# One full transpose per unit from a table that holds the weights twice, and merges in 32 pieces

## The chip, the core and the metric

The kernel is one program on one core of a Trainium2 chip. The core has five engines that run their own instruction streams and meet at semaphores: PE (TensorE, matrix products), DVE (VectorE), ACT (ScalarE), POOL (GpSimd) and SP (SyncE, which here only issues transfers). Sixteen DMA engines move data between the main memory and the core's own memory. The metric is the device time of one execution in microseconds (us). In the profile PEld is the loading of a stationary operand into PE, a queue written as POOLq or PEq is the sequencer of that engine, and `L1238` is line 1238 of the kernel's file.

## The reference, cut to what matters

Three layers follow each other over 14336 tokens of 192 numbers: a short causal convolution (softmax weights over 7 taps, one set of weights per head), a soft mixture of experts, and a sparse mixture in which every token goes to its two best of eight experts.

```python
x = attn(x, weight)                       # 7 taps per head, group of 24 columns
logits = x @ phi                          # 32 slots
slot_input = softmax_over_tokens(logits).T @ x
slot_out = relu(slot_input[e] @ w1[e]) @ w2[e]        # 8 experts, 4 slots each
x = softmax_over_slots(logits) @ slot_out             # = c @ slot_out
noisy = x @ w_gate + log1p(exp(x @ w_noise)) * noise
top2 = the two largest of the 8 per token; top2_w = their softmax
for e in range(8):                                    # second mixture
    h = relu(x[tokens of e] @ moe2_w1[e])             # 192 -> 1024
    out[tokens of e] += top2_w * (h @ moe2_w2[e])     # 1024 -> 192
```

After the first mixture a token is known by its 32 slot weights `c` alone, since `x = c @ slot_out`. The kernel uses that: `x @ moe2_w1[e]` becomes `c @ (slot_out @ moe2_w1[e])`, a product over 32 slots. To keep precision with 16-bit operands, `c` and the folded weights are each split into a high and a low half (hi, lo), so a product over 32 slots has 4 x 32 = 128 rows: hi·hi, lo·hi, hi·lo and lo·lo.

## The kernel before, in words

**Prefix (0 to about 146 us).** Eight groups of 16 x 112 tokens pass through the convolution, the transposes, the logits and the slot sums (`conv`, `trans`, `logits`, `slotsum`). The slot weights of every token stay in the tile `call` (112 partitions, 128 x 32 numbers). The small experts of the first mixture close the prefix.

**Routing of set 0 (about 146 to 188 us).** The tokens form four sets of 3584. For set 0 `route` works out, mostly on DVE, which tokens go to which expert at which place. In the middle ACT and POOL fill the tile `tab`, in four parts (`s_hi`): ACT copies the high halves from `call`, POOL subtracts for the low halves. In between ACT and POOL also fold and split the weights of the second mixture (`w1_split`, tiles `whl`, then `W1P`). `s_st` stores `tab` as rows of `table` in main memory. A row is 33 numbers: 32 numbers' worth of hi and lo halves, and one gate. Each token has two rows, one for its first and one for its second expert, with the same hi and lo and another gate.

**Units (from about 188 us).** The work on experts is cut into 238 units of 128 tokens with one expert. Each unit runs through these steps:

- `gather(i)`: POOL issues an indirect transfer that brings 128 rows of `table` (line 1183). It is issued 10 to 20 units ahead.
- `fetch(i)`: SP issues the load of the expert's first weights, 256 KB.
- `prep(i)`: PE transposes the 128 rows twice (line 1205), into PSUM partitions 0 to 63 and 64 to 127, since the 128-row product needs hi and lo twice. ACT copies the result to `ct`.
- `layer1(i)`: eight PE products (line 1214), then ACT makes the high half `hh` (line 1218) and DVE the low half `hl` (line 1219).
- `layer2(i)`: sixteen PE products, a 384-column one from `hh` (line 1227) and a 192-column one from `hl` (line 1229) in turn, then ACT and DVE scale by the gate and add (lines 1235, 1236) into one of five `o` tiles.
- POOL issues an indirect transfer that scatters `o` to one of two output arrays (line 1238): first experts to `out_0`, second experts to `out_1`, in turn.

PE, ACT, DVE, POOL and SP run their units' steps in program order. The routing of the sets 1 to 3, and of a last group MIX of partly filled units, is threaded between the units, a few DVE steps per unit by a budget. Whatever is left of a set's routing when its first gather is due is put there in one piece. The order of the units is set 0, 1, 2, MIX, 3.

**Merges.** At the end `out_1` must be added to `out_0`. POOL issues accumulating transfers from memory to memory (line 1305). Before the change there are eight, two per set, each of 1344 KB. The first six stand after the units 197, 203, 209, 215, 221 and 227; the two of set 3 stand after the last unit. Gathers, scatters and merges share POOL's instruction stream and one DMA queue. A scatter waits for the landing of the previous scatter to the same output, which is the one two units before.

Of the kernel before, what the change touches and what calls it, by code (L numbers as in the profile page):

```python
# [21 lines left out]
F32 = mybir.dt.float32  # L22
F16 = mybir.dt.float16
# [32 lines left out]
ROW = 33  # L56
CW = 32
# [9 lines left out]
MLAG, MSTEP, MPARTS = 2, 6, 2  # L67
# [21 lines left out]
def kernel(ctx, tc, xh, wraw_in, wband_in, consts_in, phi_in, w1a_in, w1b_in, w2_in, wgn_in, noise_in,  # L89
# [7 lines left out]
    table = dram.tile([2 * (NTOK + 128), ROW], F32, name="table")  # L97
# [35 lines left out]
    wrb = keep.tile([128, 4, 16], F32, name="wrb")  # L133
    ct0 = [keep.tile([128, 4 * P], F32, name=f"ct0{i}") for i in range(len(SETS[0]))]
# [110 lines left out]
    def v_split(e, half):  # L245
        w = W2[:, e * 3072:(e + 1) * 3072].rearrange("p (k d) -> p k d", k=8)[:, 4 * half:4 * half + 4]
        v = V2[e][:, 4 * half:4 * half + 4]
        t = v2t[half]
        DVE.tensor_scalar(t, v, w2s[:, e:e + 1], None, op0=OP.mult)
        if half:  # L250
            POOL.tensor_scalar(w[:, :, :D], v, w2s[:, e:e + 1], None, op0=OP.mult)
        else:
            ACT.activation(w[:, :, :D], t, AF.Copy)  # L253
        POOL.tensor_tensor(out=w[:, :, D:], in0=t, in1=w[:, :, :D], op=OP.subtract)  # L254

# [145 lines left out]
    def load_small():  # L401
        SP.dma_start(noise, noise_in)
        SP.dma_start(wgn, wgn_in)
        for o in outs:
            SP.dma_start(o[NTOK:], zero[:, :D])
        SP.dma_start(table[2 * NTOK:].rearrange("(p k) r -> p (k r)", k=2), zero[:, :2 * ROW])

# [5 lines left out]
    for g in range(NG):  # L413
        last = g == NG - 1
        conv(g, (0, 1, 2, 3))
        if g:
            tok_e(g - 1)
        if not g:
            v_stat(0)
        conv(g, (4, 5))  # L420
        if not g:
            v_max(0)
        if 0 < g < NG - 1:
            tok_l(g - 1)
        conv(g, (6, 7))
        if g + 2 < NG:
            load_x(g + 2)
        else:
            load_w1_rest(g - NG + 2)
        if g:  # L430
            v_rest(g)
            if g + 2 < NE:
                load_v(g + 2)
        trans(g, TPART[0])
        if not g:
            v_rest(0)
# [215 lines left out]
    def route(s, pool, rbank, idbank, nb):  # L652
# [46 lines left out]
        def s_hi(gl, h):  # L699
            if gl == 0 and h == 0:  # L700
                R["tab"] = pool.tile([P, TT, 2, ROW], F32, name="tab", bufs=1)
            a, b = gl * GT + h * GT // 2, gl * GT + (h + 1) * GT // 2
            tv = R["tab"].bitcast(F16)[:, a:b, :, :2 * CW].rearrange("p j c (b s) -> p j c b s", b=2)
            c2 = call[:, g0 + a:g0 + b, :].unsqueeze(2).to_broadcast([P, b - a, 2, NS])
            a = ACT.activation(tv[:, :, :, 0, :], c2, AF.Copy)
            if s:
                tc.keep_in_program_order(a)
            (DVE if s else POOL).tensor_tensor(out=tv[:, :, :, 1, :], in0=c2, in1=tv[:, :, :, 0, :], op=OP.subtract)
# [116 lines left out]
        def s_g3(i):  # L825
# [5 lines left out]
            DVE.tensor_tensor(out=R["tab"][:, :, i, CW], in0=f, in1=R["gd"][:, 2 - i], op=OP.mult)  # L831

        def s_st(gl):
            a = 2 * (TROW[s] + gl * GT * P) * ROW
            dst = bass.AP(tensor=table.tensor, offset=table.offset + a, ap=[[2 * GT * ROW, P], [1, 2 * GT * ROW]])
            SP.dma_start(dst, R["tab"][:, gl * GT:(gl + 1) * GT].rearrange("p j c w -> p (j c w)"))
# [103 lines left out]
        def s_ids():  # L940
# [11 lines left out]
            for c in range(2):  # L952
                DVE.tensor_scalar(R["row"][:, c], x[:, c, :N], 2.0, c - 2.0, op0=OP.mult, op1=OP.add)
# [51 lines left out]
    def route_mix(pool, bank):  # L1005
# [104 lines left out]
        def x_ids():  # L1110
# [7 lines left out]
            for c in range(2):  # L1118
                DVE.tensor_scalar(R["row"][:, c], a[:, c], 2.0, c - 2.0, op0=OP.mult, op1=OP.add)
# [60 lines left out]
    def gather(i):  # L1180
        s, c, u = order[i]
        RW[i] = fin.tile([128, ROW], F32, name="row", bufs=LOOK + RAMP[1] + 2)
        POOL.indirect_dma_start(out=RW[i], out_offset=None, in_=table[:2 * TEND[s]],  # L1183
# [37 lines left out]
    def layer2(i):  # L1221
# [9 lines left out]
        gv = RW[i][:, CW:]  # L1231
# [151 lines left out]
```

## Time and profile before

| what | value |
|---|---|
| time, median of 3 runs | 921.35 us (917.63 to 921.68) |
| profiled execution, its own time | 924.08 us |
| span of the profiled execution | 922.2 us |
| mean granted PE clock, of 2.4 GHz | 0.957 |
| PE busy | 841.6 us, 91% |
| DVE / ACT / POOL busy | 623.7 / 512.7 / 544.9 us |

A busy share is an average over the whole span. PE busy is close to the span because its products are pipelined and overlap in the record. POOL's 59% leaves out the gaps between its instructions. A row of the timeline gives start, duration, engine, line, the operand names, a count when rows are merged, and in square brackets the idle time before with what ended it.

### The profile page before, as it was taken

To read this page: it belongs to the slowest core of one execution; us is meant where nothing else is said; L and a number is where in the kernel's file an instruction comes from. 1 tells how busy PE (TensorE), PEld (TensorE's weight loads), DVE (VectorE), ACT (ScalarE), POOL (GpSimd) and SP (SyncE) were. 2 spreads that over 40 slices of the span, in tenths; PEclk is the share of its full clock that TensorE was granted. 3 is DMA by queue.
4 is the path that set the end of the run, shared out by engine and by line. 5 is a ranking of instruction groups with operands and counts; after the bars stand their busy time and mean duration, and the time that the engine had idled before them with its cause. 6 is when DMAs were issued, how large, how long until landed. Compare 5 with 4: busy or idle time off the path is not lost. (4 is left out here: it accounts for less than half of the span.)

```text
span 922.2 us, 25241 instructions
## 1 busy us (share of the span) xinstructions
PE 841.6 (91%) x8187; PEld 586.0 (64%) x8187; DVE 623.7 (68%) x1362; ACT 512.7 (56%) x1064; POOL 544.9 (59%) x534
## 2 busy tenths in 40 slices
PE   9999999399999999999999989999999897878960
PEld 5655544267777777776777767777776675655740
DVE  4768655959897989788989896665655564444530
ACT  5656524356577757766675535656555554444530
POOL 2354332277676767667776617777777775655431
PEclk9999999599999999999999989999999999888985
DMA  8675395643445343544364314444444346666646
GB/s 318 223 278 180 109 405 230 184 147 133 133 128 179 133 140 123 180 138 138 101 210 135 132 64 149 138 149 136 144 137 139 127 148 172 164 159 160 167 95 128
DMA packets 63702, 148.85 MB, mean 161 GB/s; under 512 B 13008, under 2 KB 20880, under 8 KB 61024
## 3 DMA queue, kind: packets, MB, share of 16 engines
q1 hardware_dynamic: 42624, 108.78, 32.0%
q0 software_dynamic: 20960, 38.46, 17.7%
q8 instruction: 79, 1.29, 0.6%
q14 instruction: 39, 0.32, 0.1%
HBM read 56.34 MB, written 39.47 MB: 104 GB/s over the span
## 5 line engine op out<-in xcount | busy, mean ns | idle before, releaser
L1227 PE MATMUL po<-W,hh 128*128 x1904 | 495.6, 330 | 24.5 <-DVE o L1236 24.4
L1229 PE MATMUL po<-W,hl 128*128 x1904 | 471.1, 249 | 0.0
L1219 DVE SCALAR_TENSOR_TENSOR hl<-ph,hh 128x1024 f16<-128x1024 f32 (+1 forms) x240 | 291.0, 1213 | 102.3 <-ACT hh L1218 100.0
L1238 POOL DMA_INDIRECT out_dram<-o,ids x238 | 240.8, 1012 | 136.5 <-DVE o L1236 65.1
L1183 POOL DMA_INDIRECT row<-table,row x238 | 232.1, 975 | 109.6 <-issue 45.1
L1218 ACT ACTIVATE hh<-ph 128x1024 f16<-128x1024 f32 (+1 forms) x240 | 243.7, 1016 | 41.2 <-PE ph L1214 16.2
L1227 PEld LDWEIGHTS <-hh 128*128 128x128 f16 x1904 | 188.1, 99 | 110.9 <-issue 5.6
L1235 ACT ACTIVATE t<-po,row 128x192 f32<-128x192 f32 x238 | 99.8, 419 | 239.8 <-PE po L1229 221.4
L1229 PEld LDWEIGHTS <-hl 128*128 128x128 f16 x1904 | 188.0, 99 | 27.8 <-issue 27.1
L1236 DVE SCALAR_TENSOR_TENSOR o<-po,row,t 128x192 f32<-128x192 f32 x238 | 98.9, 415 | 106.2 <-DMA out_dram<-o,ids 74.7
L1214 PE MATMUL ph<-ct,ws 128*128 128x128 f16 x1904 | 149.4, 222 | 1.6 <-DVE hl L1219 0.8
L1214 PEld LDWEIGHTS <-ws 128*128 128x128 f16 x1904 | 108.5, 98 | 17.7 <-issue 1.6
L1207 ACT ACTIVATE ct<-pt 128x128 f16<-128x128 f16 x238 | 64.0, 269 | 7.1 <-PE pt L1205 6.6
L254 POOL TENSOR_TENSOR W<-m,W 128x768 f16<-128x768 f32 x16 | 26.4, 1648 | 69.4 <-ACT W L253 68.7
L1205 PE MATMUL pt<-id,row 128*64 128x128 f16 x476 | 59.3, 245 | 0.2 <-DMA row<-table,row 0.2
L1205 PEld LDWEIGHTS <-row 128*64 128x64 f16 x476 | 26.2, 107 | 51.1 <-issue 38.0
L276 PE MATMUL cv<-arena,m 118*112 118x384 f32 x112 | 41.0, 495 | 0.0
L924 ACT ACTIVATE ohu<-ohu,cst 112x72 f16<-112x72 f16 x118 | 32.2, 343 | 14.7 <-DVE ohu L908 13.1
L276 PEld LDWEIGHTS cv<-arena,m 118*112 118x112 f32 x112 | 17.9, 176 | 13.7 <-issue 3.4
L293 PE MATMUL t<-cst,y 112*128 112x112 f32 x192 | 22.2, 264 | 0.6 <-ACT x1t L296 0.6
L318 ACT ACTIVATE ets<-lt,mg 128x448 f32<-128x448 f32 x8 | 5.1, 633 | 31.3 <-DVE mg L317 27.1
L282 DVE COPY y<-cv 112x384 f32<-112x384 f32 (+2 forms) x32 | 13.9, 454 | 12.3 <-PE cv L276 8.4
(327 smaller groups left out, 689.0 us busy)
## 6 DMA issues: line engine op xcount, KB each, us to landing
ws<-W1P SPq DMA_DIRECT2D x238, 256.0 KB
arena<-in_xh_dram SPq DMA_DIRECT2D x7, 1536.0 KB
out_dram<-out_dram POOLq DMA_DIRECT2D x8, 1344.0 KB
arena<-in_v_dram SPq DMA_DIRECT2D x8, 768.0 KB
arena<-in_w1a_dram SPq DMA_DIRECT2D x4, 1024.0 KB
arena<-in_v1a_dram SPq DMA_DIRECT2D x2, 2048.0 KB
row<-table,row POOLq DMA_INDIRECT x238
out_dram<-o,ids POOLq DMA_INDIRECT x238
```

The costliest lines, as they stand in the source:

```text
L276: PE.matmul(cvv, T[:, h, :], X[g][:, :, h * GC:(h + 1) * GC], start=True, stop=True)
L1183: POOL.indirect_dma_start(out=RW[i], out_offset=None, in_=table[:2 * TEND[s]], in_offset=bass.IndirectOffsetOnAxis(ap=RT[s]["row"][:, c, u ...
L1205: PE.transpose(pt[a:a + 64, :128], RW[i][:, :CW].bitcast(F16), id16)
L1207: ACT.activation(CT[i], pt[:, :128], AF.Copy)
L1214: L1[i] = PE.matmul(ph[:, k * 128:(k + 1) * 128], WS[i][:, k * 128:(k + 1) * 128], CT[i], start=True, stop=True).ins
L1218: ACT.activation(HH[i][:, s], ph[:, s], AF.Relu)
L1219: LO[i] = DVE.scalar_tensor_tensor(HL[i][:, s], ph[:, s], 0.0, HH[i][:, s], op0=OP.max, op1=OP.subtract).ins
L1227: PE.matmul(po[:, :384], HH[i][:, k * 128:(k + 1) * 128], w[:, bass.ds(r, 384)], start=k == 0, stop=False, skip_group_check=True)
L1229: last = PE.matmul(po[:, 192:384], HL[i][:, k * 128:(k + 1) * 128], w[:, bass.ds(r, 192)], start=False, stop=k == 7, skip_group_check=True)
L1235: PIN[ET.Activation] = ACT.activation(t, po[:, :D], AF.Copy, scale=gv).ins
L1236: PIN[ET.DVE] = DVE.scalar_tensor_tensor(o, po[:, D:2 * D], gv, t, op0=OP.mult, op1=OP.add).ins
L1238: POOL.indirect_dma_start(out=dst, out_offset=bass.IndirectOffsetOnAxis(ap=RT[s]["ids"][:, c, u:u + 1], axis=0), in_=o, in_offset=None)
```

## The change

**The table.** A row now has 66 numbers and there is one row per token: hi, lo, hi, lo, and both gates. The table keeps its size. The row numbers for the gathers are the token numbers, without the factor two. The gate of a unit is column `CW + c` of the row.

**The transpose.** `prep` makes one 128 x 128 transpose instead of two of 128 x 64.

**The low halves of set 0.** A new tile `hilo0` holds hi and lo of set 0. It is filled by `hi_lo` in the prefix, in the groups 2 and 3. In the routing of set 0, `s_hi` is one ACT copy per part that writes hi, lo, hi, lo, and POOL has no part in it. It stands after four of the dense steps instead of after one. For the sets 1 to 3 the number and size of the instructions of `s_hi` stay the same.

**The merges.** 32 pieces of 336 KB instead of 8 of 1344 KB: eight per set, one every 1.6 units from unit 197 on, and the eight of set 3 after the last unit.

```diff
-ROW = 33
-CW = 32
+ROW = 66
+CW = 64
-MLAG, MSTEP, MPARTS = 2, 6, 2
+MLAG, MSTEP, MPARTS = 2, 1.6, 8
+    hilo0 = keep.tile([P, NSET[0] // P, 2, NS], F16, name="hilo0")
+    def hi_lo(a, b):
+        ACT.activation(hilo0[:, a:b, 0, :], call[:, a:b, :], AF.Copy)
+        POOL.tensor_tensor(out=hilo0[:, a:b, 1, :], in0=call[:, a:b, :], in1=hilo0[:, a:b, 0, :], op=OP.subtract)
...
         if 0 < g < NG - 1:
             tok_c(g - 1)
+        if 2 <= g < 2 + len(SETS[0]):
+            hi_lo((g - 2) * GT, (g - 1) * GT)
...
+            if s == 0:
+                tv = R["tab"].bitcast(F16)[:, a:b, :2 * CW].rearrange("p j (a r) -> p j a r", a=2)
+                ACT.activation(tv, hilo0[:, a:b].rearrange("p j b s -> p j (b s)").unsqueeze(2)
+                               .to_broadcast([P, b - a, 2, 2 * NS]), AF.Copy)
+                return
...
-            (DVE if s else POOL).tensor_tensor(out=tv[:, :, :, 1, :], in0=c2, in1=tv[:, :, :, 0, :], op=OP.subtract)
+            DVE.tensor_tensor(out=tv[:, :, :, 1, :], in0=c2, in1=tv[:, :, :, 0, :], op=OP.subtract)
...
-            for c in range(2):
-                DVE.tensor_scalar(R["row"][:, c], x[:, c, :N], 2.0, c - 2.0, op0=OP.mult, op1=OP.add)
+            DVE.tensor_scalar(R["row"], x[:, :, :N], -1.0, None, op0=OP.add)
...
-            while parts and (k == 0 if s == 0 else len(parts) >= len(dense) - k):
-                add(s_hi, 0.0 if s == 0 else 0.6, *parts.pop(0))
+            while len(parts) >= len(dense) - k or (parts and s == 0 and k >= 3):
+                add(s_hi, 0.6 if s else 0.0, *parts.pop(0))
...
-            for a in (0, 64):
-                PE.transpose(pt[a:a + 64, :128], RW[i][:, :CW].bitcast(F16), id16)
+            PE.transpose(pt[:, :128], RW[i][:, :CW].bitcast(F16), id16)
...
-        gv = RW[i][:, CW:]
+        gv = RW[i][:, CW + c:CW + c + 1]
...
-            merges.setdefault(min(when, NU - 1), []).append((a + k * NSET[s] // MPARTS, a + (k + 1) * NSET[s] // MPARTS))
+            merges.setdefault(min(int(when), NU - 1), []).append((a + k * NSET[s] // MPARTS, a + (k + 1) * NSET[s] // MPARTS))
```

The change shows in the program order at three places. The first is PE, at the seam between the second layer of one unit and the first layer of another (`hl` and `hh` are the halves of the hidden numbers, `row` the gathered rows, `ws` the expert's weights). Before:

```order
L1229 MATMUL po<-W_66,hl 128x192
L1205 LDWEIGHTS row
L1205 MATMUL pt<-id_71,row 64x128
L1205 LDWEIGHTS row
L1205 MATMUL pt<-id_71,row 64x128
L1214 LDWEIGHTS ws
L1214 MATMUL ph<-ct,ws 128x128
```

Of the change, whose lines stand nine further down:

```order
L1238 MATMUL po<-W_66,hl 128x192
L1214 LDWEIGHTS row
L1214 MATMUL pt<-id_71,row 128x128
L1223 LDWEIGHTS ws
L1223 MATMUL ph<-ct,ws 128x128
```

Two loads and two products with 64 output rows became one load and one product with 128, the shape of its neighbours.

The second place is POOL in the routing of set 0, between the end of the prefix (`call`) and the first gathers (`row<-table`). Before:

```order
L353 TENSOR_TENSOR call<-call,rs 112x512 x2
L630 TENSOR_TENSOR whl<-wt,whl 128x512 x2
L708 TENSOR_TENSOR tab<-call,tab 112x16x32 x4
L630 TENSOR_TENSOR whl<-wt,whl 128x512 x2
L828 TENSOR_TENSOR u<-sb,fe 112x256
```

Of the change:

```order
L359 TENSOR_TENSOR call<-call,rs 112x512 x2
L638 TENSOR_TENSOR whl<-wt,whl 128x512 x4
L840 TENSOR_TENSOR u<-sb,fe 112x256
```

The four subtractions for `tab` left this place; two subtractions for `hilo` stand in the prefix instead.

The third place is the end of POOL's stream, from the last gather on (`out_dram<-o` are scatters, `out_dram<-out_dram` merges). Before:

```order
L1183 DMA row<-table,row_2207 128x33
L1238 DMA out_dram<-o,ids_2206 3584x192 x4
L1305 DMA out_dram<-out_dram 224x1536
L1238 DMA out_dram<-o,ids_2206 3584x192 x6
L1305 DMA out_dram<-out_dram 224x1536
L1238 DMA out_dram<-o,ids_2206 3584x192 x10
L1305 DMA out_dram<-out_dram 224x1536 x2
```

Of the change:

```order
L1193 DMA row<-table,row_2207 128x66
L1247 DMA out_dram<-o,ids_2206 3584x192 x2
L1314 DMA out_dram<-out_dram 64x1344
L1247 DMA out_dram<-o,ids_2206 3584x192
L1314 DMA out_dram<-out_dram 64x1344
...
L1247 DMA out_dram<-o,ids_2206 3584x192
L1314 DMA out_dram<-out_dram 64x1344
L1247 DMA out_dram<-o,ids_2206 3584x192 x4
L1314 DMA out_dram<-out_dram 64x1344 x8
```

Twenty scatters follow the last gather in both. Before, two merges stand among them and four stand ahead of the last gather; now ten stand among them and fourteen ahead.

## Rows read from the trace of the kernel before

**Rows 1.** Windows: stretches; busy us of each engine (instructions), granted clock, DMA share, GB/s.

```profile
194.50:527.10 332.60, 330.50 (x3347) 245.37 (x3347) 288.79 (x688) 224.64 (x480) 237.62 (x236) 1.00 0.44 144
527.10:548.75 21.65, 18.02 (x204) 13.53 (x202) 21.29 (x69) 6.55 (x12) 0.03 (x1) 0.84 0.12 44
548.75:769.00 220.25, 216.99 (x2092) 155.59 (x2091) 130.02 (x162) 129.03 (x241) 167.66 (x172) 1.00 0.43 141
769.00:844.00 75.00, 61.72 (x535) 42.97 (x533) 32.07 (x41) 33.10 (x63) 45.07 (x46) 0.89 0.67 162
844.00:902.40 58.40, 43.31 (x380) 30.26 (x377) 23.32 (x31) 22.46 (x42) 21.45 (x22) 0.90 0.54 137
```

**Rows 2.** Timeline of PE, a unit's second layer ends and another's first layer begins.

```profile
401.45 0.33 PE L1227 MATMUL po<-W,hh 128*128 x1
401.61 0.25 PE L1229 MATMUL po<-W,hl 128*128 x1
401.79 0.25 PE L1205 MATMUL pt<-id,row 128*64 128x128 f16 x2
401.96 0.62 PE L1214 MATMUL ph<-ct,ws 128*128 128x128 f16 x8
402.42 0.33 PE L1227 MATMUL po<-W,hh 128*128 x1
```

**Rows 3.** Timeline of PE around four full-width transposes of the routing (L372).

```profile
196.98 0.25 PE L1229 MATMUL po<-W,hl 128*128 x1
197.06 0.55 PE L372 MATMUL bg<-cst,call 112*128 112x112 f32 x4
197.54 0.25 PE L1205 MATMUL pt<-id,row 128*64 128x128 f16 x2
```

**Rows 4.** POOL's lines in 548.7 to 769: busy, mean ns, idle time before.

```profile
L1183 POOL DMA_INDIRECT row<-table,row x91 | 87.9, 966 | 49.1 <-ACT hh L1218 26.8 <-issue 16.2 <-ACT ct L1207 3.0
L1238 POOL DMA_INDIRECT out_dram<-o,ids x81 | 80.1, 989 | 25.2 <-issue 11.9 <-DMA out_dram<-o,ids 7.9 <-DVE o L1236 2.6
```

**Rows 5.** POOL's lines in 194.5 to 527.2.

```profile
L1238 POOL DMA_INDIRECT out_dram<-o,ids x117 | 121.6, 1039 | 52.8 <-DVE o L1236 16.8 <-DMA out_dram<-o,ids 8.7 <-issue 6.4
L1183 POOL DMA_INDIRECT row<-table,row x119 | 116.6, 979 | 42.4 <-issue 23.5 <-ACT hh L1218 7.3 <-ACT ohu L924 3.7
```

**Rows 6.** Window of the part of that stretch in which DVE is fullest.

```profile
240.00:265.00 25.00, 25.00 (x244) 18.26 (x242) 23.10 (x68) 15.74 (x32) 18.46 (x19) 1.00 0.42 138
```

**Rows 7.** Timeline of POOL around the first merge.

```profile
769.31 1.06 POOL L1305 DMA_DIRECT2D out_dram<-out_dram  x1
...
772.04 1.01 POOL L1238 DMA_INDIRECT out_dram<-o,ids  x1 [0.30 <-DVE hl L1219]
...
783.06 0.98 POOL L1238 DMA_INDIRECT out_dram<-o,ids  x1 [6.16 <-DVE o L1236]
```

**Rows 8.** Timeline of DVE, the unit that waited there.

```profile
782.37 0.42 DVE L1236 SCALAR_TENSOR_TENSOR o<-po,row,t 128x192 f32<-128x192 f32 x1 [7.93 <-DMA out_dram<-o,ids]
```

**Rows 9.** Timeline of POOL in the routing of set 0.

```profile
159.03 4.56 POOL L708 TENSOR_TENSOR tab<-call,tab 112x512 f16<-112x512 f32 x4
163.63 2.26 POOL L630 TENSOR_TENSOR whl<-wt,whl 128x512 f16<-128x512 f32 x2
```

**Rows 10.** Timeline of DVE at the same time.

```profile
162.57 1.05 DVE L785 TENSOR_SCALAR rsmi<-rsmi 128x16 int32<-128x16 int32 x1
163.66 1.15 DVE L786 CAST meta<-rsmi 128x16 f32<-128x16 int32 x1
```

**Rows 11.** Timeline of DVE, the same lines for set 1.

```profile
238.05 0.17 DVE L785 TENSOR_SCALAR rsmi<-rsmi 128x16 int32<-128x16 int32 x1
238.25 0.17 DVE L786 CAST meta<-rsmi 128x16 f32<-128x16 int32 x1
```

**Rows 12.** Timeline of POOL, the end of the program.

```profile
899.52 0.96 POOL L1238 DMA_INDIRECT out_dram<-o,ids  x1 [0.87 <-DMA out_dram<-o,ids]
902.42 1.91 POOL L1305 DMA_DIRECT2D out_dram<-out_dram  x2 [1.94 <-DMA out_dram<-o,ids]
```

More of the change, by code (lines that the diff above doesn't have):

```diff
@@ L96 @@
     dram = ctx.enter_context(tc.tile_pool(name="dram", bufs=1, space=DRAM))
-    table = dram.tile([2 * (NTOK + 128), ROW], F32, name="table")
+    table = dram.tile([NTOK + 128, ROW], F32, name="table")
     wd = [dram.tile([128, 2, F], F16, name=f"wd{i}") for i in range(2)]
@@ L405, in load_small @@
             SP.dma_start(o[NTOK:], zero[:, :D])
-        SP.dma_start(table[2 * NTOK:].rearrange("(p k) r -> p (k r)", k=2), zero[:, :2 * ROW])
+        SP.dma_start(table[NTOK:], zero[:, :ROW])
     load_w1a = [lambda i=i: SP.dma_start(W1A[i], w1a_in[:, i]) for i in range(2)]
@@ L700, in s_hi @@
             if gl == 0 and h == 0:
-                R["tab"] = pool.tile([P, TT, 2, ROW], F32, name="tab", bufs=1)
+                R["tab"] = pool.tile([P, TT, ROW], F32, name="tab", bufs=1)
             a, b = gl * GT + h * GT // 2, gl * GT + (h + 1) * GT // 2
-            tv = R["tab"].bitcast(F16)[:, a:b, :, :2 * CW].rearrange("p j c (b s) -> p j c b s", b=2)
+            if s == 0:
[3 more added lines that the diff above has]
+                return
+            tv = R["tab"].bitcast(F16)[:, a:b, :2 * CW].rearrange("p j (a b s) -> p j a b s", a=2, b=2)
             c2 = call[:, g0 + a:g0 + b, :].unsqueeze(2).to_broadcast([P, b - a, 2, NS])
-            a = ACT.activation(tv[:, :, :, 0, :], c2, AF.Copy)
-            if s:
-                tc.keep_in_program_order(a)
-            (DVE if s else POOL).tensor_tensor(out=tv[:, :, :, 1, :], in0=c2, in1=tv[:, :, :, 0, :], op=OP.subtract)
+            tc.keep_in_program_order(ACT.activation(tv[:, :, :, 0, :], c2, AF.Copy))
+            DVE.tensor_tensor(out=tv[:, :, :, 1, :], in0=c2, in1=tv[:, :, :, 0, :], op=OP.subtract)
         def s_n1():
@@ L830, in s_g3 @@
             DVE.tensor_reduce(out=f, in_=je(w), axis=AX, op=OP.add)
-            DVE.tensor_tensor(out=R["tab"][:, :, i, CW], in0=f, in1=R["gd"][:, 2 - i], op=OP.mult)
+            DVE.tensor_tensor(out=R["tab"][:, :, CW + i], in0=f, in1=R["gd"][:, 2 - i], op=OP.mult)
         def s_st(gl):
-            a = 2 * (TROW[s] + gl * GT * P) * ROW
-            dst = bass.AP(tensor=table.tensor, offset=table.offset + a, ap=[[2 * GT * ROW, P], [1, 2 * GT * ROW]])
-            SP.dma_start(dst, R["tab"][:, gl * GT:(gl + 1) * GT].rearrange("p j c w -> p (j c w)"))
+            a = (TROW[s] + gl * GT * P) * ROW
+            dst = bass.AP(tensor=table.tensor, offset=table.offset + a, ap=[[GT * ROW, P], [1, GT * ROW]])
+            SP.dma_start(dst, R["tab"][:, gl * GT:(gl + 1) * GT].rearrange("p j w -> p (j w)"))
         def steps_of(acc, vals, off1, w, op=OP.is_le):
@@ L1117, in x_ids @@
             DVE.tensor_tensor(out=a, in0=a, in1=b, op=OP.add)
-            for c in range(2):
-                DVE.tensor_scalar(R["row"][:, c], a[:, c], 2.0, c - 2.0, op0=OP.mult, op1=OP.add)
+            DVE.tensor_scalar(R["row"], a, -1.0, None, op0=OP.add)
             DVE.tensor_scalar(b, a, NTOK - NLAST + 0.5, -float(NTOK), op0=OP.is_gt, op1=OP.mult)
@@ L1182, in gather @@
         RW[i] = fin.tile([128, ROW], F32, name="row", bufs=LOOK + RAMP[1] + 2)
-        POOL.indirect_dma_start(out=RW[i], out_offset=None, in_=table[:2 * TEND[s]],
+        POOL.indirect_dma_start(out=RW[i], out_offset=None, in_=table[:TEND[s]],
                                 in_offset=bass.IndirectOffsetOnAxis(ap=RT[s]["row"][:, c, u:u + 1], axis=0))
```

## The prediction

> **What bounds the kernel now.** I read the busy shares first, and they mislead: PE is busy 91% of the span, so every step taken off PE seems to count. Then I cut the unit phase into stretches with the windows view, because the routing, the wait for MIX and the merges each have a stretch of their own [rows 1]. The timeline of PE gives the price of a unit, and the grouped lines of POOL show how full its stream is.
>
> From 194.5 to 527.1 PE is busy almost without a break, DVE 288.8 of 332.6 us (87%), and POOL carries 117 scatters and 119 gathers. They take 121.6 + 116.6 busy and 52.8 + 42.4 between [rows 5]. Three engines are near their limit at once.
>
> From 527.1 to 548.75 POOL does nothing. The first gather of MIX waits for the routing, and DVE is full, 21.29 of 21.65 [rows 1].
>
> From 548.75 to 769 POOL is the bound, although its busy time is only 167.66 of 220.25. Its 91 gathers and 81 scatters take 87.9 + 80.1, and 74.3 lies between them [rows 4]. Of that, 21.65 is the wait above, which ends this window's first idle gap. What is left, 52.7, is 0.31 behind each of 172 instructions. So an instruction takes 1.28 with its gap, and 172 x 1.28 = 220 is the whole stretch. The reader is to see that a gap that stands behind each instruction is no free time. PE is also busy there 216.99 of 220.25, so the two engines are nearly in step.
>
> From 769 to 902.4 come the merges. Of 133.4 us PE is busy 105, at a granted clock of 0.89 to 0.90 [rows 1]. A scatter waits for the landing of the one two before it, and behind the first merge the scatter of 772.04 has landed only at 782.3, when DVE and then POOL go on after 7.93 and 6.16 us of waiting [rows 7, 8].
>
> **The transpose.** PE starts the last L1229 at 401.61, the pair of transposes at 401.79, the eight L1214 at 401.96 and the next L1227 at 402.42 [rows 2]. A 192-column product is followed after 0.08 elsewhere [rows 3], so 0.10 of the first 0.18 is a gap. The pair takes 0.17 more. A unit is seven pairs L1227 and L1229 at about 0.245, one L1227 at 0.16 and this seam of 0.81, together 2.69. Four transposes of full width, L372, show more: they begin 0.08 after the L1229 ahead, with no gap, and the next narrow pair comes 0.48 after their start [rows 3]. They read 32-bit numbers, so their own pace is no measure for 16 bits. I take the pace of L1214, 0.46 for eight, that is 0.06. The new seam is 0.08 + 0.06 + 0.46 = 0.60, the unit 2.48, the gain 0.21 per unit on PE. The bounds are 0 (the gap belongs to a transpose of gathered rows of any width) and 0.21.
>
> The Trainium skill speaks against this in "TensorE: Matmul & The Clock Gate", Part 4, PE-mode transpose: a full 16-bit transpose took about 275 ns in one kernel's context. By that figure the new seam would be as long as the old one. The trace has 0.48 for the four of L372 together, so I give it a chance as a rival and not the forecast.
>
> Now stretch by stretch, against the execution of 924.08 (span 922.2).
>
> **Routing of set 0.** POOL's four subtractions, 4.56 us, go [rows 9]. While they and the next two run, small DVE steps wait: L785 and L786 take 1.05 and 1.15 [rows 10], against 0.17 each for set 1 [rows 11]. That is 1.9 us on DVE, which sets the pace there. On ACT the four copies write twice as much and so hold back the second pair of `whl`, and this pair will then meet other small DVE steps. Bounds 0 and -3.5, the latter if all DVE steps beside the removed ones become short; I take -1.5. The two new ACT copies and POOL subtractions in the prefix I cost at nothing: ACT there waits for DVE once per group. Uncovered they cost four instructions of about 1 us, or +2 on the path (the four on POOL take 1.14 each [rows 9]).
>
> **194.5 to 527.1.** PE would give back 117 x 0.21 = 25. POOL can give back less: 236 x 0.31 of its 95.2 idle must stay, so at most 95.2 - 73.2 = 22. DVE in its fullest quarter is busy 23.10 of 25 [rows 6], so 7.6% at most, about what PE would take there. Lower bound 0, upper bound 22. With three engines in series of small buffers I take 60% of the upper bound, -13.
>
> **527.1 to 548.75.** The same DVE steps are left over when MIX's first gather is due, since they are handed out per unit. 0.
>
> **548.75 to 769.** POOL has the same 172 instructions. A gather of 264 bytes a row is the same instruction with as many rows, and I cost it as before. PE becomes faster and waits more. 0, with a lower bound of -20 if POOL's gap shrinks.
>
> **769 to 902.4.** Of 112 gathers from MIX on, 21 are left at 769 (112 - 91), with as many scatters up to the last gather. That is 42 x 1.28 = 53.8. Fourteen merge pieces stand in this part now instead of four. A whole merge holds POOL 1.06 [rows 7], a scatter of 128 rows 1.01, so size hardly counts and I take 1.05 each: 14.7. POOL reaches the last gather 68.5 after 769.3. Does a scatter still stall? The landing took 10.3 behind a whole merge (772.04 to 782.3). At the end it took at most 2.9 (899.52 to 902.42) [rows 12]. The merge therefore adds about 7.4 and a quarter 1.9, so a scatter behind a piece lands after 4.8. The scatter two later is issued 4 x 1.28 + 1.05 = 6.2 after it, so there is no stall. Bounds for all pieces: 0, and 6 x 6.2 = 37 if six waits like that one stay [rows 7].
>
> The Trainium skill gives a fixed price that speaks against small pieces, in "DMA: Bandwidth & Descriptors", Anatomy of one DMA, SWDGE path: about 2.0 us per transfer beside its bytes. If these added up, 24 more pieces would cost 48 us. Two merges are issued in one run of 1.91, without a wait for the first to land [rows 12], and I do not add them.
>
> After the last gather PE can be five units ahead of the scatters (five `o` tiles), so 15 units are left: 15 x 2.48 = 37.2. POOL needs 20 x 1.28 + 10 x 1.05 = 36.1, nearly the same. Then one scatter must be issued and land: product to `o` 1.0, landing 2.9, together 4. The last merges are issued 68.5 + 37.2 + 4 = 109.7 after 769.3, or at 879.0 against 902.42: -23.4.
>
> **The end.** The same bytes in eight pieces. POOL issues one in about 1, a quarter of a merge moves in more. 0, bounds -0.5 and +2.
>
> **Sum.** -1.5 - 13 - 23.4 = -37.9, or 886 for the profiled execution. This stood 2.7 above the median of the runs, so 883.
>
> **Rivals.**
>
> *VectorE holds the first sets.* With 87% and up to 92% busy, DVE gives back only 3 there. For it: the small steps meet POOL's instructions. Against: its mean leaves 43 us. 924.1 - 1.5 - 3 - 23.4 - 2.7 = 894.
>
> *The gap at the transpose stays.* Then 194.5 to 527.1 gives 0, and at the end PE needs 15 x 2.69 = 40.4, so -20.2 there. 924.1 - 1.5 - 20.2 - 2.7 = 900. Against it are the gapless L372. The figure of the Trainium skill's Part 4, named above, would bring this case about.
>
> *POOL is not the bound.* If its gaps shrink when work waits, PE's pace holds everywhere: -25, then 81 x 2.48 = 201 for 220, then 36 units x 2.48 + 4 for 133.1. 924.1 - 1.5 - 25 - 19 - 40 - 2.7 = 836. Against it: 0.31 is the same behind gathers and scatters over 172 instructions.
>
> *The stalls stay.* If pieces delay scatters as whole merges do, the last part gives 0: 924.1 - 1.5 - 13 - 2.7 = 907.
>
> *Slower: PE falls to its lower clock while the merges run.* POOL then needs 2.57 + 0.66 = 3.2 per unit (1.05 per 1.6 units), PE 2.48, so PE rests 0.7 in each unit. Now its granted clock in 769 to 902.4 is 0.9 of the full, 2.4 GHz, with falls to 1.2 behind stops of several us. If it stayed at 1.2 for these 36 units, they would take 36 x 4.96 + 4 = 183 instead of 133, +50, and with the 14.5 gained before 957. It decides from the point where more than 14.5 + 23.4 us are lost, some 15 units at the lower clock. Against it: from 548.75 to 769 PE also waits again and again and its clock is 1.00.
>
> **How the numbers follow.** Forecast 0.64 (its own range 872 to 893, from the bounds of the first sets and of the routing), DVE 0.13, gap stays 0.10, POOL not the bound 0.05, stalls stay 0.04, lower clock 0.04. The range 868 to 903 takes in the forecast, DVE and the gap, and leaves out some 0.17. A measurement of this kernel can tell about 0.5%, 4.6 us. All cases but the last are faster by more: faster 0.95, same 0.015, slower 0.035.
>
> **What would show it.** The seam of 0.81 should be about 0.60 from L1238 to the next L1236 of the changed file, with no gap before the transpose. From MIX's first gather to the first merge POOL should again be saturated, and the stretch should last 220 us. L797 and L798 should take about 0.17. POOL should have no wait of 5 us or more behind a merge, 3.2 us per unit while it still gathers, and PE's clock should stay full there. The prediction is wrong if that saturated stretch shortens (POOL's price was wrong), if the first sets do not change (DVE or the gap), or if POOL waits behind pieces.

## The result and the profile after

The changed kernel takes 889.43 us (median of 4 runs, 888.87 to 891.38) where the kernel before takes 920.97: a ratio of 0.967, 95% interval 0.964 to 0.970. Forecast were 883 and a range of 868 to 903. The profiled execution took 891.38 with a span of 889.6, against 924.08 and 922.2, so the sum can be checked stretch by stretch:

| from ... to | before | forecast | after |
|---|---|---|---|
| start, first unit (first `t`) | 194.6 | 193.1 | 193.2 |
| first unit, MIX's first gather | 354.2 | 341.2 | 333.7 |
| MIX's first gather, first merge | 220.6 | 220.6 | 220.8 |
| first merge, last gather | 73.6 | 68.5 | 67.8 |
| last gather, last merges | 59.5 | 41.2 | 53.1 |
| last merges, end of the span | 19.8 | 19.8 | 21.0 |
| sum | 922.2 | 884.3 | 889.6 |

Two rows are off, in opposite directions: the first sets gained 20.4 instead of 13, and behind the last gather 6.4 was gained instead of 18.3. The experiments turn mainly on these two.

The windows of the changed kernel, cut at its own events, answer to [rows 1], whose first two lines together are the first one here (length; busy us and instructions of PE, weight loads, DVE, ACT, POOL; granted clock, DMA share, GB/s):

```profile
193.10:526.90 333.80, 324.89 (x3431) 257.01 (x3429) 304.84 (x751) 221.90 (x493) 249.36 (x237) 0.99 0.47 152
526.90:747.70 220.80, 207.27 (x2027) 159.58 (x2025) 127.24 (x165) 124.70 (x243) 167.93 (x172) 1.00 0.46 147
747.70:816.60 68.90, 58.67 (x537) 44.17 (x535) 31.56 (x41) 32.69 (x66) 54.68 (x56) 0.93 0.82 185
816.60:868.60 52.00, 34.24 (x322) 26.01 (x321) 21.27 (x29) 18.82 (x36) 28.92 (x30) 0.94 0.70 147
868.60:889.60 21.00, 0.00 (x0) 0.00 (x0) 0.00 (x0) 0.00 (x0) 6.54 (x8) 0.50 0.70 131
```

In the second line POOL has the same 172 instructions in the same time as in [rows 1], although PE has lost 10 us of busy time. In the fourth PE is busy for 34 of 52 and POOL for 29, or about 35 with the 0.30 that stands ahead of each scatter: neither is the bound, so something else is.

The seam of PE, in its timeline, against [rows 2]:

```profile
402.04 0.25 PE L1238 MATMUL po<-W,hl 128*128 x1
402.12 0.22 PE L1214 MATMUL pt<-id,row 128*128 128x128 f16 x1
402.17 0.61 PE L1223 MATMUL ph<-ct,ws 128*128 128x128 f16 x8
402.62 0.33 PE L1236 MATMUL po<-W,hh 128*128 x1
...
404.50 0.25 PE L1238 MATMUL po<-W,hl 128*128 x1
```

From L1238 to L1236 it is 0.58 (0.81 before), the unit 404.50 - 402.04 = 2.46 (2.69). The gap of 0.10 ahead of the transpose is gone, as for L372 in [rows 3].

POOL's lines up to the last scatter ahead of MIX (193.1 to 505.7), against [rows 5]:

```profile
L1247 POOL DMA_INDIRECT out_dram<-o,ids x116 | 124.3, 1071 | 38.0 <-issue 8.8 <-DMA out_dram<-o,ids 6.7 <-DVE hl L1228 6.3
L1193 POOL DMA_INDIRECT row<-table,row x118 | 120.9, 1025 | 37.6 <-issue 23.4 <-ACT hh L1227 4.6 <-ACT ct L1216 4.0
```

The idle time is 75.6, and 234 x 0.31 = 72.5 of it is the gap that stands behind each instruction. Before it was 95.2. POOL now runs without a pause here too. (The mean of 1071 for the scatters holds one of 8.80 us, at 504.59, where the gathers stop for MIX; without it the mean is 1.00 us.)

The timeline of POOL behind the last gather (the bracket is the idle time before and what the profile names as its end):

```profile
815.53 1.06 POOL L1193 DMA_INDIRECT row<-table,row  x1 [0.31 <-issue]
816.89 1.01 POOL L1247 DMA_INDIRECT out_dram<-o,ids  x1 [0.30 <-issue]
819.31 0.99 POOL L1247 DMA_INDIRECT out_dram<-o,ids  x1 [1.41 <-DVE o L1245]
820.32 0.94 POOL L1314 DMA_DIRECT2D out_dram<-out_dram  x1
823.38 1.02 POOL L1247 DMA_INDIRECT out_dram<-o,ids  x1 [2.12 <-DVE o L1245]
...
831.16 1.02 POOL L1247 DMA_INDIRECT out_dram<-o,ids  x1 [1.42 <-DVE o L1245]
```

These waits are put down to DVE's `o`, and that name misleads. The scatter of 823.38 is unit 220's. DVE had begun its `o` at 810.82 and was done at 811.23, 12.1 us earlier:

```profile
810.82 0.42 DVE L1245 SCALAR_TENSOR_TENSOR o<-po,row,t 128x192 f32<-128x192 f32 x1 [1.94 <-DMA out_dram<-o,ids]
```

What came last is the scatter two before, issued at 816.89: its last bytes moved at 821.19 by the times of the single DMA packets in the trace. In all units from 219 on the `o` was ready 6.0 to 12.9 us before its scatter, and the scatter followed 1.1 to 3.2 us (median 2.05) after the last byte of the one two before. So a chain of landings sets the pace. DVE shows the other side:

```profile
822.67 0.42 DVE L1245 SCALAR_TENSOR_TENSOR o<-po,row,t 128x192 f32<-128x192 f32 x1 [2.51 <-DMA out_dram<-o,ids]
```

This is the `o` of unit 223. All five `o` tiles are full, so DVE, and PE behind it, wait for the same landings: PE is five units ahead, and it can't use that.

### The profile page after: what moved, and what is told of

Read it like the earlier page. It is cut to its first block, busy times and chain, and to the rows that moved or that the text cites. A ratio compares the mean times of both kernels' runs of the same rounds, so it can differ in the third digit from the quotient of the medians.

```text
span 889.6 us, 24797 instructions
## 1 busy us (share of the span) xinstructions
PE 795.6 (89%) x7949; PEld 584.7 (66%) x7949; DVE 612.6 (69%) x1357; ACT 497.7 (56%) x1066; POOL 575.9 (65%) x556
## 5 line engine op out<-in xcount | busy, mean ns | idle before, releaser
L1236 PE MATMUL po<-W,hh 128*128 x1904 | 496.4, 328 | 28.2 <-DVE o L1245 27.3
L1238 PE MATMUL po<-W,hl 128*128 x1904 | 469.1, 247 | 0.0
L1247 POOL DMA_INDIRECT out_dram<-o,ids x238 | 245.4, 1031 | 92.7 <-issue 27.4
L1193 POOL DMA_INDIRECT row<-table,row x238 | 240.6, 1011 | 92.0 <-issue 46.3
L1236 PEld LDWEIGHTS <-hh 128*128 128x128 f16 x1904 | 187.0, 98 | 109.5 <-issue 4.3
L1238 PEld LDWEIGHTS <-hl 128*128 128x128 f16 x1904 | 186.8, 98 | 38.3 <-issue 35.0
L1223 PE MATMUL ph<-ct,ws 128*128 128x128 f16 x1904 | 145.4, 219 | 1.6 <-DVE hl L1228 0.9
L1223 PEld LDWEIGHTS <-ws 128*128 128x128 f16 x1904 | 116.6, 98 | 2.6 <-issue 2.0
L1214 PE MATMUL pt<-id,row 128*128 128x128 f16 x238 | 52.2, 219 | 2.5 <-DMA row<-table,row 2.3
L936 ACT ACTIVATE ohu<-ohu,cst 112x72 f16<-112x72 f16 x118 | 32.2, 343 | 24.4 <-DVE ohu L920 22.6
L1214 PEld LDWEIGHTS <-row 128*128 128x128 f16 x238 | 23.6, 99 | 17.3 <-DMA row<-table,row 5.6
L1314 POOL DMA_DIRECT2D out_dram<-out_dram x32 | 28.7, 1160 | 2.0 <-DMA out_dram<-o,ids 1.9
```

The costliest lines, as they stand in the source:

```text
L1214: PE.transpose(pt[:, :128], RW[i][:, :CW].bitcast(F16), id16)
L1223: L1[i] = PE.matmul(ph[:, k * 128:(k + 1) * 128], WS[i][:, k * 128:(k + 1) * 128], CT[i], start=True, stop=True).ins
L1236: PE.matmul(po[:, :384], HH[i][:, k * 128:(k + 1) * 128], w[:, bass.ds(r, 384)], start=k == 0, stop=False, skip_group_check=True)
L1238: last = PE.matmul(po[:, 192:384], HL[i][:, k * 128:(k + 1) * 128], w[:, bass.ds(r, 192)], start=False, stop=k == 7, skip_group_check=True)
L1247: POOL.indirect_dma_start(out=dst, out_offset=bass.IndirectOffsetOnAxis(ap=RT[s]["ids"][:, c, u:u + 1], axis=0), in_=o, in_offset=None)
```

## The experiments

The runs of e5 and e6 were on a chip on which the kernel before takes 921.08, as in the result. The others ran on three chips on which it takes 1097 to 1100, so there I compare only stretches of kernels on such chips. The column "us" holds medians; the stretches are of the profiled execution, each from where the one before it ends. Here the last one starts at the last scatter, and without merges the stretches around the first merge are blank. "u" is the time of a unit from 219 to 237, from `t` to `t`.

| run | us (before) | ratio, 95% | first unit to MIX | to first merge | to last gather | to last scatter | to end | u |
|---|---|---|---|---|---|---|---|---|
| before | 920.97 | | 354.2 | 220.6 | 73.6 | 56.6 | 22.7 | 3.22 |
| after | 889.43 (920.97) | 0.964 to 0.970 | 333.7 | 220.8 | 67.8 | 50.2 | 23.9 | 2.86 |
| e5 | 911.35 (921.08) | 0.986 to 0.993 | 355.8 | 220.3 | 66.8 | 47.2 | 24.5 | 2.88 |
| e6 | 882.13 (921.08) | 0.955 to 0.961 | 333.7 | 208.6 | 99.0 | 20.2 | 24.3 | 2.99 |
| e1 | 1097.0 (1100.4) | 0.993 to 1.002 | 449.7 | 296.5 | 72.8 | 52.9 | 22.6 | 2.55 |
| e2 | 1092.9 (1100.4) | 0.990 to 1.000 | 450.2 | 301.6 | 69.3 | 48.4 | 24.6 | 2.72 |
| e3 | 1071.7 (1100.4) | 0.967 to 0.984 | 445.9 | | | 50.0 | 6.5 | 2.47 |
| e4 | 1089.5 (1100.4) | 0.987 to 0.995 | 442.5 | 298.5 | 69.1 | 50.4 | 23.5 | 2.82 |
| e7 | 1092.8 (1099.1) | 0.992 to 1.001 | 449.0 | 288.3 | 106.8 | 24.6 | 22.6 | 3.08 |
| e8 | 1099.1 (1099.1) | 0.996 to 1.004 | 460.9 | 292.1 | 74.6 | 51.0 | 22.6 | 2.54 |
| e9 | 1072.7 (1099.1) | 0.969 to 0.989 | 448.5 | | | 49.5 | 6.5 | 2.44 |
| e10 | 1095.5 (1097.5) | 0.994 to 1.004 | 443.7 | 294.5 | 68.1 | 39.5 | 38.7 | 2.56 |
| e11 | 1073.9 (1097.5) | 0.973 to 0.982 | 443.4 | | | 48.1 | 6.6 | 2.41 |
| e12 | 1094.5 (1097.5) | 0.994 to 1.002 | 447.4 | 297.4 | 72.2 | 51.4 | 22.6 | 2.50 |

**The pair of narrow transposes back (e2, e5).**

```
-            PE.transpose(pt[:, :128], RW[i][:, :CW].bitcast(F16), id16)
+            for a in (0, 64):
+                PE.transpose(pt[a:a + 64, :128], RW[i][:, :CW // 2].bitcast(F16), id16)
```

> The kernel of e2_two_narrow once more, on a chip where the kernel before takes about 921, as the theories of e2 presume. Theory A (the seam of PE is the gain of the first sets, POOL's 1.28 us per instruction is the bound behind MIX's first gather): from the first unit to MIX's first gather 354 instead of 333.7, from there to the first merge 221 as it is, the time 908 to 914. Theory B (the gain came from the gathers or the routing): 889 to 893. Theory C (POOL is not the bound behind MIX's first gather): both stretches grow and the time passes 920. On a chip like that of e1 to e4 no theory says anything.

The same kernel on the first of the slower chips, where its time and first stretches say nothing:

> The changed kernel with the pair of 64-column transposes back, both from the first half of the wide row. Theory A (the seam of PE is the gain of the first sets, POOL's 1.28 us per instruction is the bound behind MIX's first gather): the seam L1238 to L1236 goes from 0.60 to 0.81, the stretch from the first unit to MIX's first gather from 333.7 to about 354, the one from there to the first merge stays at 221 though PE is slower there as well, the merge stretch grows by 0 to 4, the time is 910 to 914. Theory B (the gain of the first sets came from the gathers or the routing, not from the transpose): 889 to 893. Theory C (POOL is not the bound behind MIX's first gather): that stretch grows too, by up to 18, and the time passes 920.

Theory A, as put for e5, held in its stretches and its time. What the text of e2 adds, a merge stretch longer by 0 to 4, did not come. Windows of e5, the first three stretches:

```profile
194.90:550.60 355.70, 349.04 (x3547) 259.00 (x3546) 310.13 (x752) 231.28 (x492) 238.12 (x236) 0.99 0.44 143
550.60:770.90 220.30, 216.51 (x2087) 155.40 (x2084) 130.33 (x162) 128.97 (x240) 167.93 (x172) 1.00 0.45 147
770.90:838.80 67.90, 60.01 (x569) 42.59 (x568) 32.87 (x43) 35.41 (x66) 54.70 (x56) 1.00 0.86 193
```

The first sets go back to 355.8, the stretch of the 172 instructions stays at 220.3 with a unit of 2.69 on PE as with one of 2.46. So the whole transpose is worth 911.35 - 889.43 = 21.9, which the first sets alone give (22.1), and the rest of the change 9.7. In the merge stretch the slower PE does no harm: 116.9 from the first merge to the last ones, against 120.9 for the changed kernel and 133.1 before, in one profile each. So the merge stretch's gain does not come from PE's shorter units. Of what else changed, the pieces alone act on the merges, so I put it down to them.

**Without the extra gathers (e6).**

```
-RAMP = (140, 10, 4)
+RAMP = (140, 0, 4)
```

> The changed kernel without the ten extra gathers ahead that start at unit 140 (RAMP 0 instead of 10): ten gathers move from the stretch that POOL bounds to the last units, where PE does. Theory A (POOL's instructions are the bound until the last gather, the last units are held by landings behind pieces and by PE): the stretch from MIX's first gather to the first merge shrinks by up to 10 x 1.28, and with gathers between them the last scatters stand farther apart than pieces delay their landing: the time falls by 8 to 13 to about 878. Theory B (PE or DMA hold those stretches): no change, 887 to 891. Theory C (PE starves for rows when gathers are only nine ahead of the pieces): slower, above 895.

The setting also cuts the buffers of `row` from 21 to 11. The time is 882.13, 7.3 less than the changed kernel and a little short of A's 8 to 13; the two intervals of the ratio don't overlap (0.955 to 0.961, 0.964 to 0.970), and this is the fastest version found. Its windows:

```profile
527.30:735.90 208.60, 204.48 (x2024) 157.53 (x2022) 129.61 (x165) 125.95 (x243) 158.49 (x162) 1.00 0.47 154
735.90:835.90 100.00, 80.77 (x754) 60.04 (x753) 49.34 (x61) 48.20 (x90) 80.56 (x82) 0.97 0.80 182
835.90:857.90 22.00, 11.90 (x110) 8.87 (x108) 6.98 (x10) 5.76 (x11) 13.64 (x15) 0.86 0.59 121
```

Ten POOL instructions fewer in the first of these lines shorten it by 12.2 = 10 x 1.22. That shows that POOL's stream of instructions is the bound there. From the first merge to the last ones the time is about the same, 122.0 for 120.9, although ten gathers more lie in it: beside the gathers the scatters wait less. Of POOL's waits there 3.9 us are put down to `o` and 2.7 to a landing; in the changed kernel's merge stretch 17.9 and 4.4. So the gain of the first line is kept; what A had hoped for at the end did not come on top.

**The ten late pieces behind the last scatter (e10, beside e4).**

```
-            merges.setdefault(min(int(when), NU - 1), []).append(
+            merges.setdefault(int(when) if when < 218 else NU - 1, []).append(
```

> The changed kernel with the ten pieces that stood among the last 20 scatters moved behind the last scatter, so that 18 are issued there instead of 8. Theory A (the scatters behind the last gather wait for landings that pieces delay): from the last gather to the last scatter 37 to 39 instead of 49.2, the end from the last merges on grows from 21.0 by ten times about 2, the time is 896 to 902 where the changed kernel takes 889.4. Theory B (these units are slow for another reason): 49 stays there and the time is about 910. On a chip like that of e1 to e4 the two stretches alone count.

Windows of e4, with the pieces among the scatters, behind its last gather:

```profile
1011.90:1064.10 52.20, 37.23 (x341) 27.96 (x338) 22.37 (x30) 19.97 (x39) 28.92 (x30) 0.90 0.70 152
1064.10:1084.70 20.60, 0.00 (x0) 0.00 (x0) 0.00 (x0) 0.00 (x0) 6.53 (x8) 0.50 0.70 134
```

and of e10:

```profile
1008.20:1047.60 39.40, 35.48 (x345) 27.28 (x342) 22.17 (x30) 20.51 (x39) 19.43 (x20) 1.00 0.35 112
1047.60:1085.40 37.80, 0.00 (x0) 0.00 (x0) 0.00 (x0) 0.00 (x0) 14.51 (x19) 0.51 0.85 166
```

From the last gather to the last scatter 39.5 instead of 50.4 on chips of the same kind (A: 37 to 39, B: 49), and from unit 231 on each `o` was scattered within 0.9 us of being written. The forecast's 41.2, the last landing included, comes out as 40.5 without the pieces (1007.13 to 1047.65). The clock hardly differs: up to PE's last product it is 0.96 in e4 and 1.00 in e10, and the 0.90 of e4's first line takes in a fall behind that product. The run moves a piece's bytes and its 0.9 to 1.0 of POOL's stream together, so it does not price the two apart; that the scatters wait for landings is what the packets show. Behind the last scatter the ten pieces cost 15, more than the 11 that they had cost among the scatters, so their place was not wrong; the forecast's price for them was.

**No merges (e3, e9, e11).** The add of the two halves of the output is left out.

```
-            POOL.dma_start(outs[0][a:b], outs[1][a:b], accum_op=OP.add, max_dma_last_dim=6144)
+            if a < 0:
+                POOL.dma_start(outs[0][a:b], outs[1][a:b], accum_op=OP.add, max_dma_last_dim=6144)
```

> The changed kernel without any merge: the two halves of the output are not added. It prices the pieces. Theory A (behind the last gather the scatters wait for landings that pieces delay): from the first unit of the last set the time to the last gather falls from 67.8 to about 54 (14 x 1.25 less), from there to the last scatter from 50 to about 38 (15 x 2.46 and 1), and the time is about 847, with the bytes at the end gone. Theory B (the last 20 units are slow for another reason, PE's clock or the queue of weights): the part from the last gather to the last scatter stays at 49 to 50 and the time is about 858.

> The kernel of e3 once more, on a chip where the kernel before takes about 921: no merge at all, the two halves of the output are not added. On the other chip the units 219 to 237 took 2.47 each without pieces and 2.82 with them. Theory A (the scatters behind the last gather wait for landings that pieces delay): from the last gather to the last scatter 37 to 39 instead of 49.2, from the first unit of the last set on POOL is saturated up to the last gather, the time is 845 to 850. Theory B (the last units are slow for another reason): 49 there and 857 to 860.

> The kernel of e3 and e9, no merge at all (the two halves of the output are not added), for a chip where the kernel before takes about 921. Theory A: from the last gather to the last scatter 37 to 39 instead of 49.2 and, ahead of it, 54 instead of 67.8 for the same gathers, the time 845 to 850. Theory B: 49 stays, 857 to 860.

All three were on the slower chips, and the number named, from the last gather to the last scatter, came out as 48 to 50, as B says. But B's reason was not there. Without pieces PE isn't ahead at the last gather on these chips (a scatter follows its `t` within 1.1 to 2.1 us), so 20 units lie behind it and not 15, at 2.41 to 2.47 each, PE's own pace. With ten pieces among them the same units take 2.72 to 2.88 (e2, e4, e5 and the changed kernel). The runs don't tell A from B by the number I had chosen; e10 does, where PE was ahead as in the changed kernel.

**The merges of before in the changed kernel (e1, e8, e12).**

```
-MLAG, MSTEP, MPARTS = 2, 1.6, 8
+MLAG, MSTEP, MPARTS = 2, 6, 2
```

> The changed kernel with the merges of before (two pieces per set, six units apart). Theory A (the 32 pieces are worth what the merge stretch gained, and the faster units of PE nothing there, since POOL and the landings hold it): the stretch from the first merge to the last ones goes back from 120.9 to about 133, the stretches ahead of it stay at 333.7 and 220.8, the time is about 901. Theory B (the merge stretch gained by PE's shorter units, the pieces are worth nothing): 888 to 892. Theory C (with PE faster the whole merges stall more than before): above 905.

> The kernel of e1 once more, on a chip where the kernel before takes about 921: the changed kernel with the merges of before (two pieces per set, six units apart). Theory A (the pieces are worth what the merge stretch gained): the stretch from the first merge to the last ones is about 133 instead of 120.9, those ahead of it stay at 333.7 and 220.8, the time is about 901. On the other chip the stretch was 128.7, which would give 897. Theory B (the merge stretch gained by PE's shorter units): 888 to 892. Theory C (the whole merges stall more with the faster PE): above 905. On a chip like that of e1 to e4 only the merge stretch says anything.

> The kernel of e1 and e8, the changed kernel with the merges of before, for a chip where the kernel before takes about 921. On two other chips the stretch from the first merge to the last ones took 128.7 and 128.5 us, with pieces (e4) 122.4. Theory A: 128 to 133 instead of 120.9, the time 896 to 901. Theory B: 888 to 892. Theory C: above 905.

Only the merge stretch counts here: 128.7, 128.5 and 126.5 with whole merges, 122.4 (e4) and 120.6 (e2) with pieces on such chips. The direction is A's, the size 4 to 8. On its quicker chip e5, which has the old pace of PE, gives 133.1 - 116.9 = 16 for all of the change but the transpose, the pieces above all. The changed kernel with whole merges was not seen on such a chip, so how much of 12.2 it would lose stays open. The wait behind a whole merge is still there, in e8's timeline of POOL:

```profile
1004.60 0.98 POOL L1193 DMA_INDIRECT row<-table,row  x1 [0.31 <-issue]
1010.56 0.98 POOL L1247 DMA_INDIRECT out_dram<-o,ids  x1 [4.99 <-DVE o L1245]
```

**Four larger pieces per set (e7).** On top of e6:

```
-MLAG, MSTEP, MPARTS = 2, 1.6, 8
+MLAG, MSTEP, MPARTS = 2, 3.2, 4
```

> The kernel of e6 with four pieces of 672 KB per set, one every 3.2 units, instead of eight of 336 KB every 1.6. Theory A (a piece costs POOL's stream about 1.25 whatever its size, and a landing behind 672 KB, 2.9 + 3.8 = 6.7, is just longer than the 6.4 between a scatter and the one two later): 12 pieces fewer, 15 less for POOL, some 3 to 5 given back by stalls, the time is 869 to 873. Theory B (the bytes of a merge hold the queue, not the number of pieces): the stalls grow as the pieces do, 880 to 884. Theory C (whole-merge stalls come back): above 885.

It ran on a slower chip, so its time says nothing. The timeline of POOL shows a wait behind a 672 KB piece:

```profile
990.73 0.99 POOL L1314 DMA_DIRECT2D out_dram<-out_dram  x1
...
997.26 0.97 POOL L1193 DMA_INDIRECT row<-table,row  x1 [0.30 <-issue]
999.76 0.99 POOL L1247 DMA_INDIRECT out_dram<-o,ids  x1 [1.53 <-issue]
```

Ten pieces stand ahead of the last gather, and ten times a scatter came 2.1 to 4.8 after the gather ahead of it, 3.2 on the mean, instead of 1.28. In e6, with 20 smaller pieces there, it was once over 2 (2.09). A loss of 1.9 for each larger piece is more than the 1.25 that A says it saves: B rather than A. On such chips a scatter also comes late where there is no piece at all, up to 5.1 behind its gather in e3, e9 and e11, but there its `o` was ready only 0.3 before; in the ten cases of e7 it was ready 1.1 to 10.8 before, so these wait for a landing. What they would cost on a chip like that of e6 is not settled.

**The low halves made in the routing again (e4).**

```
-            if 2 <= g < 2 + len(SETS[0]):
-                hi_lo((g - 2) * GT, (g - 1) * GT)
...
+            (DVE if s else POOL).tensor_tensor(out=tv[:, :, :, 1, :], in0=c2, in1=tv[:, :, :, 0, :], op=OP.subtract)
```

> The changed kernel with the low halves of the first set made by POOL in the routing, as before. Theory A (POOL's work beside the small steps costs what the routing gained): the first unit starts about 1.4 to 2.2 later, the small steps L797 and L798 take about 1 us again, the time is 890.5 to 892. Theory B (the routing's gain came from elsewhere): 888 to 890, with no later first unit.

DVE in e4's routing (the lines are renumbered: L793 and L784 are L798 and L789 of the changed kernel):

```profile
163.67 1.03 DVE L793 CAST meta<-rsmi 128x16 f32<-128x16 int32 x1
164.74 1.15 DVE L784 TENSOR_TENSOR_SCAN meta<-zero,meta 128x8 f32<-128x8 f32 x2
```

and the changed kernel:

```profile
162.82 0.17 DVE L797 TENSOR_SCALAR rsmi<-rsmi 128x16 int32<-128x16 int32 x1
163.03 0.17 DVE L798 CAST meta<-rsmi 128x16 f32<-128x16 int32 x1
163.23 0.25 DVE L789 TENSOR_TENSOR_SCAN meta<-zero,meta 128x8 f32<-128x8 f32 x2
```

The small steps beside POOL's subtractions are slower, as A says, by 1.8 us over the two lines in e4. The first unit is nevertheless no later: at 200.8 in e4, and at 199.8, 200.6 and 201.2 in e1 to e3, which share the new routing. The trace shows why. The routing begins with ACT's first `ex`, in e4 and in e1 at

```profile
147.75 0.28 ACT L702 ACTIVATE ex<-r 112x128 f32<-112x128 f32 x1 [8.75 <-PE r L698]
149.10 0.28 ACT L704 ACTIVATE ex<-r 112x128 f32<-112x128 f32 x1 [8.74 <-PE r L700]
```

In the nine runs besides e4 on such chips, e1 among them, it begins at 149.1 to 150.0, so without the additions in the prefix it begins 1.4 to 2.2 earlier. From there to the first `t` e4 takes 53.0, the others 50.6 to 52.0. What the routing gains, the prefix takes back, on these chips and in one profile of e4.

## Why the prediction was right, and where it was not

*The seam.* 0.58 for 0.60, a unit of 2.46 for 2.48, and no gap ahead of the transpose. The Trainium skill gives about 275 ns for it in one kernel ("TensorE: Matmul & The Clock Gate", Part 4, PE-mode transpose). L1214 takes 219 ns on the mean here, but the next instruction starts 0.05 after it: a duration, not the price in a stream. The rival of the gap that stays is refuted by this and by e5.

*The routing.* -1.5 was forecast for the first unit, -1.4 measured, and this agreement is partly luck. From the first Exp of the routing to the first `t` it is 44.3, 45.4 and 44.5 in the three profiles (after, e5, e6) on quicker chips, against 46.5: a gain of 1.1 to 2.2. But the routing begins 0.8 to 1.4 later than before, and e4 shows that the two additions in the prefix do it. The step that failed is "The two new ACT copies and POOL subtractions in the prefix I cost at nothing". In sum the first unit comes 1.4 and 0.9 earlier in two of the three profiles and 0.3 later in e5.

*The first sets.* The step that failed is "I take 60% of the upper bound, -13". The stretch gave -20.4 of at most 22. The bound itself was the right one: 75.6 of idle time is left where 72.5 must stay, so POOL's stream is full. PE is busy 306.23 of the 310.10 us up to 503.2, so it has little left to give either. DVE, one of the three engines for whose series I took the discount, is busy 91% of that time and did not hold it back. The wait for MIX is as long as before, as forecast: the gathers stop from 524.9 to 548.8 before, and from 503.2 to 526.9, with one between, after. With a bound worked out to 22 and PE offering 25, the number should have been near the bound.

*MIX's first gather to the first merge.* 0 forecast, +0.3 measured, and e6 shows why: 10 instructions fewer, 12.2 less. The rival of POOL not being the bound is refuted.

*The merges up to the last gather.* 68.5 forecast, 67.8 measured, 14 pieces. No scatter waits 5 us, so the rival of the stalls that stay is refuted as well.

*Behind the last gather.* Here 41.2 was forecast and 53.1 measured. The step that failed is "a scatter behind a piece lands after 4.8. The scatter two later is issued 4 x 1.28 + 1.05 = 6.2 after it, so there is no stall". That holds as long as two gathers stand between. Behind the last gather the distance is 2 x 1.28 + 1.05 = 3.6, and the same 4.8 is now late. I had asked the question for one part and taken the answer for both. The landing was mis-sized too: a piece's bytes were taken at 1.9, and move in 2.0 only at the end, where nothing else runs; among scatters and weights they need 2.4 to 5.4 (median 3.6, by the DMA packets). From one scatter to the one two later it is 3.5 to 6.7, on the mean 48.9 / 19 x 2 = 5.1, above PE's 4.92 for two units. So the landings lead, and PE's five units in hand are never used up: its last product ends at 857.21, 8.5 us before the last scatter is issued. e10 takes the pieces away and gets 39.5.

*The end.* 0 forecast with +2 as a bound; +1.2. The fixed 2.0 us per transfer that the Trainium skill gives ("DMA: Bandwidth & Descriptors", Anatomy of one DMA) was rightly not added for pieces in a row. The same section puts most of it down to completion, the time behind the last byte; with that the trace does not agree. From the last scatter (865.75) to the first piece (868.63), which waits for its landing, it is 2.88: by the DMA packets 1.53 up to the first byte, 0.44 for the bytes and 0.91 behind the last. Eight pieces are then issued in one run:

```profile
865.75 0.96 POOL L1247 DMA_INDIRECT out_dram<-o,ids  x1 [0.30 <-issue]
868.63 6.54 POOL L1314 DMA_DIRECT2D out_dram<-out_dram  x8 [1.92 <-DMA out_dram<-o,ids]
```

All three parts are paid where one transfer waits for another, as in the chain of scatters.

*The clock.* I had asked for a full clock; the windows give 0.93 and 0.94 in the merge stretch, above the 0.89 to 0.90 of before. The fourth line, cut at PE's last product, reads:

```profile
816.60:857.20 40.60, 34.24 (x322) 26.01 (x321) 20.86 (x28) 18.40 (x35) 24.06 (x25) 1.00 0.77 161
857.20:868.60 11.40, 0.01 (x1) 0.00 (x0) 0.42 (x1) 0.42 (x1) 4.85 (x6) 0.70 0.44 97
```

So the clock is full as long as PE works there, and the slow last units are not the clock's doing. In the third line it falls to 1.2 GHz three times (at 756.0, 779.9 and 797.0), each time at the end of a stop of PE of 2.4 to 3.0 us; a stop of 2.7 at 816.4 brought no fall. The rival of the lower clock is refuted.

*The range and the total.* The forecast's own range, 872 to 893, does not follow from the bounds named: with nothing gained in the first sets it would reach 896. In all the first sets gave 7.4 more than forecast, the last units and the end 11.9 + 1.2 less. That the total came within 6.4 us of the forecast is in part luck: two of its terms were wrong in opposite directions.

## What to carry to other kernels

Once a stream's floor per instruction was known, the stretch with a faster neighbour went close to that floor here: the bound was the better forecast, and a discount needs an engine that is itself full. A "no stall" that rests on the distance between two dependent transfers has to be worked out again wherever that distance changes, here where the gathers end. And instructions moved from the stretch in which their engine is the bound to one in which it waits are a gain by themselves (e6). A mean clock over a window that runs on behind PE's last product says nothing of the products. And the name that the profile gives to a wait has to be held against the time at which that instruction ended.

## What the runs showed that was not expected

On three of the four chips that ran the experiments the kernel before takes 1097 to 1100 instead of 921, and all variants lie close together. The prefix is nearly the same (first unit at 200 instead of 194), and the last units without merges run at PE's own 2.41 to 2.47; but while POOL gathers a unit takes 3.6 to 3.9, where it takes 2.6 to 2.7 in the changed kernel and in e6 on quicker chips. From the page of e9, two of its costliest groups:

```profile
L1227 ACT ACTIVATE hh<-ph 128x1024 f16<-128x1024 f32 (+1 forms) x240 | 245.3, 1022 | 164.9 <-remote 109.6
L1236 PEld LDWEIGHTS <-hh 128*128 128x128 f16 x1904 | 194.2, 102 | 178.8 <-issue 87.0
```

In the changed kernel on its chip:

```profile
L1227 ACT ACTIVATE hh<-ph 128x1024 f16<-128x1024 f32 (+1 forms) x240 | 243.7, 1016 | 9.0 <-PE ph L1223 6.5
L1236 PEld LDWEIGHTS <-hh 128*128 128x128 f16 x1904 | 187.0, 98 | 109.5 <-issue 4.3
```

The waits end on `issue`, for which the profile shows nothing waited for, and on `remote`, which is none of the instructions recorded for this core. What it is stays open; on such a chip the full transpose, worth 22 us elsewhere, can't be told from nothing: from the first unit to MIX e1, with it, takes 449.7 and e2, without it, 450.2.
